# Cosformer attention and a token mixer: twenty products on constant data in six gaps of TensorE, and PSUM banks handed out anew

## The chip, the cores and the metric

One core of a Trainium2 chip. The metric is device time in microseconds (us) of one execution; lower is better. Times in this text count from the start of the profiled span.

## The reference

Two stages, one after the other, on 8 batches, 8 heads, 576 positions and 64 columns a head.

```python
def phi(x, c, s):
    r = np.maximum(x, 0.0)
    return np.concatenate([r * c, r * s], axis=-1)
q_p = phi(q, cos_w, sin_w)
k_p = phi(k, cos_w, sin_w)
kv = np.einsum('bhsf,bhsd->bhfd', k_p, v)
z = np.sum(k_p, axis=2)
num = np.einsum('bhsf,bhfd->bhsd', q_p, kv)
den = np.einsum('bhsf,bhf->bhs', q_p, z)[..., None] + 1e-06
...
wq = x @ w_q
wk = x @ w_k
W_tok = scale * np.einsum('bsd,btd->bst', wq, wk)
mixed = np.einsum('bst,btd->bsd', W_tok, x)
return (np.maximum(mixed, 0.0) @ w_out).astype(np.float32)
```

`x` is `num / den` with the heads side by side: 576 x 512 a batch. `cos_w` and `sin_w` depend on the position alone.

## The kernel before

The kernel has one written-out schedule, the string `ORDER` (lines 37 to 106). Each word is an operation with its arguments, then `@`, then the engine: T is TensorE (PE), V VectorE (DVE), A ScalarE (ACT), G GpSimd (POOL), Y SyncE (SP). For T the number after the letter is the first PSUM bank. `run` (line 440) goes through the words and calls the function of that name. An engine executes its own words in this order; between engines, the framework adds semaphores where one operation needs data or a buffer from another. So the string sets each engine's queue and the banks, and the data sets the rest.

The work is cut by H = 2b + h (b the batch, h one half of its eight heads, so H runs from 0 to 15) and by s, one of the two head pairs in such a half; g = 2H + s numbers the 32 head pairs. A word's numbers are H and s, or g, or b and a part of it. The steps:

- LD (line 203): loads one pair of k, q or v, 288 KB each, into one of four raw buffers, all from SP. It waits until the operation that read that buffer four halves earlier is done.
- RK (224) and MK (229): relu of k, then the product with cosine and sine (DVE). CV (237) casts v, DQ (242) makes relu of q twice side by side (POOL).
- QK (254): 18 products of k' with v and a column of ones, then 18 transposes of q, into two banks. EK (275) copies the first to SBUF, EQ (278) multiplies the second by cosine and sine; both on DVE.
- NM (288): 10 products of q' with kv. RC (299) is the reciprocal of the denominator, XN (307) the division; both on DVE.
- XT (318) and EX (331): 20 transposes of x, and their copy.
- A batch then goes through WQK, EW, DW, TK, EWK, KX, EKX, MX, EMX (lines 339 to 403: the mixer's products and the copies that read them), WO and EO (409, 417: the last product, four of 512 columns each, and its copy), and ST (422), the store. LW and CW (211, 218) load and cast the weights.

Ahead of all this stand 14 products of a constant tile `warm` (set to 1.0, line 451) with itself, 128 x 128 by 128 x 512, into bank 7, whose result nobody reads (lines 452 and 453).

TensorE's eight banks are shared by all operations: QK, NM, XT, WQK and MX take two banks, TK, KX and WO one. An operation has to wait until the last reader of its banks is done.

The start of TensorE's queue is QK.0, QK.1, NM.0, QK.3, NM.3, QK.2, QK.5, NM.1, NM.2, XT.1, NM.5, QK.4, XT.0, QK.6, NM.4, WQK.0, XT.2, TK.0, QK.7, QK.11, NM.6, KX.0, NM.7, and four MX. DVE's part beside it is EQ.0, EK.0, MK.1.1, EQ.1, RC.0, EK.1, EQ.3, EK.3, XN.0, MK.2.0, MK.2.1, RC.3, EQ.2, EK.2, XN.3, EK.5, RC.2, RC.1, XN.2, EQ.5, XN.1, MK.3.0, MK.3.1, EQ.4, EK.4, RC.5, EK.6, RC.4, MK.5.1, XN.4, XN.5.

Of the kernel before, what the change touches and what calls it, by code (L numbers as in the profile page):

```python
# [44 lines left out]
NM.2@T4 LW.qk@Y EK.5@V DQ.2.0@G RC.2@V RC.1@V LD.v.5.1@Y XN.2@V CV.3.0@G EQ.5@V LD.q.5.1@Y
XT.1@T2 XN.1@V LD.q.5.0@Y RK.3.0@A NM.5@T0 QK.4@T4 RK.3.1@A MK.3.0@V LD.k.5.0@Y XT.0@T6 CV.3.1@A
MK.3.1@V EX.1@A LD.v.4.0@Y EQ.4@V LD.q.4.0@Y EK.4@V RK.5.1@A RC.5@V QK.6@T2 LD.v.5.0@Y EX.0@A
NM.4@T4 EK.6@V CW.qk@G LD.q.4.1@Y RC.4@V RK.4.0@A MK.5.1@V WQK.0@T6 LD.k.4.1@Y CV.5.1@A DQ.3.1@G
XN.4@V LD.v.4.1@Y XN.5@V EW.0@A DQ.5.1@G LW.o@Y EQ.6@V DW.0@A XT.2@T0 TK.0@T4 LD.k.6.0@Y
MK.4.0@V QK.7@T6 EX.2@A QK.11@T2 EWK.0@V CV.4.0@G LD.k.6.1@Y EK.7@V EQ.7@V NM.6@T4 RK.5.0@G  # L50
LD.q.6.0@Y KX.0@T0 RC.6@V DQ.5.0@G XN.6@V NM.7@T6 LD.v.6.0@Y EKX.0@A CV.5.0@A DQ.4.0@G MX.0.2@T0
RC.7@V LD.k.7.0@Y MX.0.3@T4 EQ.11@V EMX.0.3@A EK.11@V LD.q.6.1@Y EMX.0.2@A MK.5.0@V MX.0.0@T4
MX.0.1@T2 RK.4.1@A QK.8@T0 LD.v.7.0@Y CV.4.1@G XN.7@V EMX.0.0@A DQ.4.1@G EQ.8@V EMX.0.1@A
XT.3@T6 QK.10@T4 EK.8@V EX.3@A MK.4.1@V NM.8@T0 EQ.10@V QK.9@T2 CW.o.0@G CW.o.1@A LD.v.6.1@Y
EK.10@V WQK.1@T6 EQ.9@V LD.q.7.0@Y RK.6.0@G EK.9@V NM.10@T4 RC.8@V LD.k.7.1@Y EW.1@A MK.6.0@V
WO.0.2@T2 LD.k.8.1@Y DQ.6.0@G RC.10@V NM.9@T6 XN.8@V EO.0.2@A WO.0.1@T3 LD.v.8.0@Y RK.6.1@A
XN.10@V CV.6.0@G TK.1@T2 EO.0.1@A LD.v.7.1@Y RK.7.0@G RC.9@V QK.12@T0 EWK.1@A XN.9@V DQ.6.1@G
LD.q.7.1@Y NM.11@T4 WO.0.0@T2 RC.11@V LD.k.8.0@Y MK.6.1@V KX.1@T3 EO.0.0@A LD.q.8.0@Y MK.7.0@V
DW.1@A WO.0.3@T6 CV.6.1@G EQ.12@V LD.k.9.0@Y EKX.1@A CV.7.0@A DQ.7.0@G MX.1.1@T2 EK.12@V
LD.v.10.0@Y XN.11@V EO.0.3@A QK.13@T0 EMX.1.1@A RK.7.1@G MX.1.0@T6 LD.k.9.1@Y QK.14@T4 EQ.13@V  # L60
EMX.1.0@A RK.8.1@G XT.4@T2 LD.v.8.1@Y EK.13@V EK.14@V MX.1.2@T6 MK.7.1@V WO.1.1@T0 EMX.1.2@A
LD.q.9.0@Y MK.8.1@V EX.4@A NM.12@T6 LD.q.8.1@Y WO.1.2@T1 DQ.7.1@G EQ.14@V EO.1.1@A LD.q.9.1@Y
RC.12@V XT.5@T2 CV.7.1@A RK.8.0@G XN.12@V NM.13@T4 LD.v.9.0@Y EX.5@A WO.1.0@T0 CV.8.0@G RC.13@V
DQ.8.0@G LD.k.10.1@Y XN.13@V MX.1.3@T6 RK.9.0@A QK.15@T2 LD.k.10.0@Y MK.8.0@V EO.1.2@A WQK.2@T4
EO.1.0@A MK.9.0@V LD.q.10.0@Y EMX.1.3@A CV.10.0@G EQ.15@V NM.14@T0 LD.v.9.1@Y EW.2@A QK.16@T6
RK.9.1@G RC.14@V CV.8.1@A EK.15@V LD.q.10.1@Y TK.2@T4 XN.14@V NM.15@T2 EWK.2@A WO.1.3@T5 DW.2@A
DQ.8.1@G LD.k.12.0@Y EQ.16@V EK.16@V LD.q.11.1@Y XT.6@T0 RC.15@V DQ.9.1@G QK.17@T6 EX.6@A
XN.15@V LD.k.11.1@Y KX.2@T4 CV.9.0@G EQ.17@V XT.7@T2 RK.10.1@G EKX.2@A EK.17@V EO.1.3@A EX.7@V
DQ.9.0@G MX.2.1@T0 NM.17@T6 EMX.2.1@A MX.2.0@T4 RC.17@V WQK.3@T2 EMX.2.0@A MK.9.1@V RK.10.0@A
CV.9.1@G XN.17@V MX.2.2@T0 QK.18@T4 EW.3@A LD.k.14.0@Y MK.10.1@V WO.1.4@T6 EMX.2.2@A ST.1.0.0@Y  # L70
MK.10.0@V LD.v.11.1@Y MX.2.3@T0 QK.19@T2 DW.3@G EQ.18@V ST.1.1.1@Y EMX.2.3@A TK.3@T7 DQ.10.0@G
EK.18@V ST.0.0.0@Y EK.19@V EWK.3@A NM.16@T0 EQ.19@V EO.1.4@A NM.18@T4 ST.1.0.1@Y WO.2.1@T7
DQ.10.1@G RC.16@V RC.18@V LD.k.11.0@Y XN.16@V QK.20@T2 ST.0.0.1@Y EO.2.1@A DQ.11.1@G XN.18@V
RK.12.0@A LD.v.10.1@Y KX.3@T0 RK.11.1@A CV.11.1@G LD.q.11.0@Y EQ.20@V NM.19@T4 EKX.3@A
LD.v.11.0@Y XT.8@T6 EK.20@V RC.19@V MX.3.1@T0 ST.0.1.0@Y EX.8@A MK.12.0@V WO.2.0@T2 LD.v.12.0@Y
XN.19@V RK.11.0@G WO.2.3@T3 LD.k.12.1@Y EMX.3.1@A MK.11.1@V ST.1.1.0@Y EO.2.0@A MX.3.2@T4
XT.9@T0 MK.11.0@V LD.v.12.1@Y QK.23@T6 EO.2.3@A LD.q.12.0@Y CV.10.1@G EX.9@V EMX.3.2@A NM.20@T2
ST.0.1.1@A DQ.11.0@G EK.23@V MX.3.3@T4 EQ.23@V WQK.4@T0 CV.11.0@A LD.q.13.1@Y RC.20@V EMX.3.3@A
LD.q.12.1@Y XN.20@V QK.22@T6 EW.4@A QK.21@T4 LD.k.13.0@Y EQ.22@V TK.4@T0 MX.3.0@T2 EK.21@V
RK.12.1@G ST.1.2.1@A WO.2.2@T1 EK.22@V EQ.21@V EWK.4@A LD.k.13.1@Y NM.23@T6 EMX.3.0@A MK.12.1@V  # L80
NM.22@T4 LD.v.13.1@Y EO.2.2@A KX.4@T0 RC.23@V RK.14.0@G CV.12.0@A XN.23@V NM.21@T2 ST.1.2.0@Y
DQ.12.0@G EKX.4@A WO.3.3@T1 RC.22@V LD.q.13.0@Y RC.21@V CV.12.1@G XN.22@V WO.3.0@T0 EO.3.3@A
LD.v.13.0@Y XN.21@V DW.4@A XT.11@T4 DQ.12.1@G ST.2.0.0@Y QK.24@T6 EX.11@V MX.4.2@T2 LD.q.14.0@Y
WO.3.2@T1 EMX.4.2@A EQ.24@V RK.13.0@G EO.3.0@A LD.v.14.0@Y EK.24@V MX.4.0@T2 MK.14.0@V QK.25@T4
EMX.4.0@A LD.k.15.0@Y MX.4.3@T6 RK.13.1@G WO.3.1@T0 EK.25@V EO.3.2@A EQ.25@V DQ.13.1@G
LD.k.14.1@Y EMX.4.3@V XT.10@T2 EO.3.1@A ST.2.0.1@Y MX.4.1@T4 WO.3.4@T1 MK.13.0@V EMX.4.1@A
ST.3.1.0@Y MK.13.1@V NM.24@T6 EO.3.4@A WO.4.0@T0 LD.v.15.0@Y CV.13.0@G RC.24@V EX.10@A XN.24@V
DQ.13.0@G NM.25@T4 LD.q.15.0@Y WO.4.1@T1 RC.25@V EO.4.0@A LD.k.15.1@Y CV.13.1@G XN.25@V QK.26@T2
EO.4.1@A DQ.14.0@G LD.q.14.1@Y QK.27@T6 CV.14.0@A EQ.26@V XT.12@T0 LD.v.14.1@Y RK.15.0@A
QK.28@T4 EK.26@V EK.27@V EX.12@A EQ.27@V RK.14.1@G ST.3.2.1@Y WQK.5@T2 EK.28@V LD.q.15.1@Y  # L90
MK.14.1@V WO.4.2@T6 EW.5@A MK.15.0@V ST.2.1.0@Y NM.27@T0 DW.5@G EQ.28@V EO.4.2@A NM.26@T2
TK.5@T7 CV.15.0@G RC.27@V EWK.5@A NM.28@T4 RC.26@V DQ.15.0@G WO.4.3@T6 XN.27@V RK.15.1@A RC.28@V
KX.5@T7 XN.26@V EO.4.3@A DQ.14.1@G QK.30@T0 EKX.5@A ST.4.1.1@Y XN.28@V MX.5.3@T2 MX.5.1@T6
LD.v.15.1@Y CV.14.1@G EQ.30@V EMX.5.3@A XT.13@T4 ST.4.1.0@Y EMX.5.1@A EK.30@V QK.29@T2 EX.13@V
ST.3.0.1@Y ST.2.1.1@A DQ.15.1@G MX.5.0@T0 NM.30@T6 EK.29@V ST.3.0.0@Y EMX.5.0@A EQ.29@V WQK.6@T4
ST.4.0.1@Y ST.3.1.1@A RC.30@V MK.15.1@V WO.5.0@T0 ST.3.2.0@Y EW.6@A XN.30@V CV.15.1@G ST.4.0.0@Y
NM.29@T2 DW.6@G TK.6@T1 RC.29@V MX.5.2@T4 QK.31@T6 EWK.6@V EMX.5.2@A XN.29@V KX.6@T1 EO.5.0@A
EK.31@V WO.5.4@T4 EQ.31@V ST.5.0.0@Y EKX.6@V NM.31@T2 ST.5.0.1@Y MX.6.0@T0 RC.31@V MX.6.1@T6
EMX.6.0@A WO.5.2@T5 XN.31@V EO.5.4@A EMX.6.1@V XT.14@T0 EO.5.2@A XT.15@T2 WO.5.3@T4 EX.14@V
EX.15@V WO.6.0@T5 EO.5.3@A WQK.7@T0 ST.5.2.0@A ST.5.2.1@Y EO.6.0@V WO.6.1@T2 EW.7@V MX.6.3@T4  # L100
DW.7@G MX.6.2@T0 EO.6.1@A TK.7@T3 EMX.6.2@V WO.5.1@T6 EWK.7@A ST.6.0.1@Y EMX.6.3@A ST.6.0.0@A
KX.7@T7 EO.5.1@V WO.6.3@T0 EKX.7@V ST.5.1.0@A ST.5.1.1@Y MX.7.1@T2 MX.7.3@T4 MX.7.0@T6 EMX.7.1@A
WO.6.2@T1 EMX.7.0@V EO.6.3@A EMX.7.3@V MX.7.2@T2 EO.6.2@A WO.7.1@T6 EMX.7.2@A ST.6.1.0@Y
WO.7.2@T7 ST.6.1.1@A EO.7.1@V WO.7.4@T0 EO.7.2@A WO.7.3@T1 ST.7.1.0@Y ST.7.1.1@A EO.7.4@V
# [404 lines left out]
```

## Time and profile before

| what | value |
|---|---|
| median of 13 runs | 132.45 us (130.33 to 134.48) |
| the profiled execution: its time, its span | 134.1 us, 132.3 us |
| TensorE (PE) busy | 104.5 us, 79% |
| VectorE (DVE) busy | 106.6 us, 81% |
| ScalarE (ACT) busy | 77.5 us, 59% |
| GpSimd (POOL) busy | 69.9 us, 53% |
| mean granted clock of TensorE | 0.912 of full |
| DMA | 39.40 MB, 298 GB/s on average |
| the 14 opening products | 1.45 to 7.25 us |

How to read it: the profile is one execution. The page cuts the span into 40 slices of 3.3 us; a digit is a busy share in tenths, and in the row PEclk the clock that TensorE was granted, in tenths of the full one. A time line row is the start, the time taken, the engine, line and operation, how many, and in square brackets how long the engine was idle before and what ended it. A row of the table of stages is a stretch of time with each engine's busy time in it, then the granted clock, the share of time that the DMA engines were busy, and GB/s. A row of waits names the engine and line that waited, the one that it waited for, the us in total, the times and the longest.

### The profile page before, as it was taken

The numbers are of one execution on the slowest core, as the hardware profiler recorded it, in microseconds if no ns is written. First come the engines' busy times: TensorE is split into PE (matmuls) and PEld (weight loads), VectorE is DVE, ScalarE is ACT, GpSimd is POOL, SyncE is SP. The second block draws the span as 40 slices with busy tenths as digits, with TensorE's granted clock in tenths as the row PEclk, the third lists the DMA queues.
The fourth block names the chain that finished last, engine by engine and source line by source line (L and its number), as shares of the span: only waits on it lengthen the run. The fifth ranks groups of instructions, "written<-read, shape, count | busy, mean of one in ns | idle before, by whom it ended". The sixth has DMA issues, their size and how long they took to land.

```text
span 132.3 us, 5180 instructions
## 1 busy us (share of the span) xinstructions
PE 104.5 (79%) x2181; PEld 69.7 (53%) x2198; DVE 106.6 (81%) x227; ACT 77.5 (59%) x124; POOL 69.9 (53%) x81
## 2 busy tenths in 40 slices
PE   5937695949789988869999869399998959999900
...
DVE  3648999798899999999999874999998967865500
...
PEclk9995555586899999999999999999999999999995
DMA  4999999999999999970299999999994998059793
GB/s 128 322 396 402 392 388 360 361 390 389 384 394 390 385 387 388 387 266 0 68 265 307 318 376 341 366 306 340 353 352 171 279 262 244 18 185 281 181 282 104
DMA packets 20711, 39.40 MB, mean 298 GB/s; under 512 B 3280, under 2 KB 3280, under 8 KB 20688
## 3 DMA queue, kind: packets, MB, share of 16 engines
...
q8 instruction: 17, 0.28, 0.9%
...
## 4 chain that ended last, share of the span: by engine, by line
DVE 35%; PE 30%; DMA 10%; SPq 8%; issue 6%; ACT 3%; POOL 2%; ACTq 2%; POOLq 0%
DVE kp L232 13%; PE banks L413 9%; DVE qpt L279 8%; DVE xs L309 7%; DMA kf<-in_k_dram 6%; SPq L208 5%; PE banks L260 4%; PE banks L292 4%; DMA qf<-in_q_dram 4%; PE banks L269 4%; PE banks L371 3%; SPq L430 3%; DVE rec L305 3%; DVE kvs L187 2%; PE banks L326 2%
## 5 line engine op out<-in xcount | busy, mean ns | idle before, releaser
L195 POOL TENSOR_SCALAR qd<-qf 128x1152 bf16<-128x1152 f32 x32 | 39.6, 1247 | 11.9 <-DMA qf<-in_q_dram 11.0
L413 PE MATMUL banks<-wo_sb,mix 128*128 128x512 bf16 x127 | 33.9, 380 | 1.3 <-issue 0.6
L232 DVE TENSOR_TENSOR kp<-rk,cossin 128x1152 bf16<-128x1152 bf16 x32 | 29.6, 944 | 2.7 <-POOL rk L195 2.3
L185 ACT COPY osb<-banks 128x512 f32<-128x512 f32 x31 | 18.0, 589 | 14.4 <-PE banks L413 9.2
L309 DVE TENSOR_TENSOR xs<-banks,rec 128x640 bf16<-128x640 f32 x32 | 25.4, 807 | 0.3
L279 DVE TENSOR_TENSOR qpt<-banks,cst 128x1152 bf16<-128x1152 bf16 x32 | 23.8, 745 | 1.9 <-PE banks L269 1.7
L401 ACT ACTIVATE mix<-banks 128x640 bf16<-128x640 f32 (+1 forms) x27 | 17.4, 656 | 10.3 <-PE banks L388 10.1
L260 PE MATMUL banks<-vb,kp 64*128 64x65 bf16 x576 | 16.7, 202 | 4.8 <-POOL vb L189 1.4
L292 PE MATMUL banks<-kvs,qpt 128*128 128x65 bf16 x320 | 16.5, 205 | 3.0 <-DVE kvs L187 2.1
L413 PEld LDWEIGHTS <-mix 128*128 128x128 bf16 x144 | 12.2, 98 | 12.5 <-issue 1.4
L269 PE MATMUL banks<-ident,qd 64*128 64x64 bf16 x576 | 16.3, 203 | 2.5 <-POOL qd L195 2.5
L260 PEld LDWEIGHTS <-kp 64*128 64x128 bf16 x576 | 13.3, 101 | 8.7 <-issue 4.3
L292 PEld LDWEIGHTS <-qpt 128*128 128x128 bf16 x320 | 14.1, 104 | 7.0 <-DVE qpt L279 2.1
L189 POOL TENSOR_SCALAR vb<-vf 128x576 bf16<-128x576 f32 x17 | 12.6, 741 | 6.6 <-DMA vf<-in_v_dram 5.5
L193 ACT ACTIVATE rk<-kf 128x576 bf16<-128x576 f32 x15 | 10.1, 684 | 9.1 <-DMA kf<-in_k_dram 7.4
L195 POOL TENSOR_SCALAR rk<-kf 128x576 bf16<-128x576 f32 x14 | 10.9, 782 | 7.7 <-DMA kf<-in_k_dram 6.5
L269 PEld LDWEIGHTS <-qd 64*128 64x128 bf16 x576 | 13.0, 103 | 2.6 <-POOL qd L195 2.6
L185 ACT COPY xT<-banks 128x1280 bf16<-128x1280 bf16 x10 | 12.3, 1226 | 3.5 <-PE banks L326 3.5
L326 PE MATMUL banks<-ident,xs 64*128 64x64 bf16 x320 | 7.9, 196 | 6.2 <-DVE xs L309 6.2
L185 ACT CAST vb<-vf 128x576 bf16<-128x576 f32 x14 | 9.4, 673 | 5.3 <-DMA vf<-in_v_dram 5.0
L189 POOL TENSOR_SCALAR wq<-wqk 64x576 bf16<-64x576 bf16 x4 | 3.0, 744 | 15.8 <-ACT wqk L185 8.0
L326 PEld LDWEIGHTS <-xs 64*128 64x128 bf16 x320 | 6.4, 99 | 9.3 <-DVE xs L309 6.1
...
## 6 DMA issues: line engine op xcount, KB each, us to landing
...
```

What stands on the lines that cost most here:

```text
L185: A.copy(dst, src)
L189: eng.tensor_scalar(dst, src, 1.0, 1.0, op0=ALU.mult, op1=ALU.mult)
L195: eng.tensor_scalar(dst, src, FMAX, 0.0, op0=ALU.min, op1=ALU.max)
L232: eng.tensor_mul(kp[H % N_KP][:, lo:hi], rk[H % N_RK][:, lo:hi].unsqueeze(3).to_broadcast([P, n, C9, 2, D]), cossin.unsqueeze(1).to_broadc ...
L260: T.matmul(kvp[:, hh, :], kp[H % N_KP][p0:p0 + 64, i, c, :, :], vb[H % N_VB][p0:p0 + 64, i, c, 0:D + 1], start=(c == 0), stop=(c == C9 - 1))
L269: T.transpose(qt[:, hh, c * D:(c + 1) * D], src, ident[p0:p0 + 64, p0:p0 + 64])
L279: eng.tensor_mul(qpt[g % N_QPT][:, :, 1:SLOTS, :], qk_views(at["QK", g])[0].rearrange("f h (c d) -> f h c d", c=C9), cst.unsqueeze(1).to_b ...
L292: T.matmul(nv[:, hh, u, :], qpt[g % N_QPT][:, hh, 2 * u:2 * u + 2, :], kvs[g % N_KV][:, hh, :], start=(u == 0), stop=(u == SC - 1 and not ...
L309: eng.tensor_tensor(xs[b % N_XS][:, :, 2 * pr:2 * pr + 2, :].rearrange("p u h d -> p h u d"), num_view(at["NM", g])[:, :, :, 0:D], rec[g % ...
L326: T.transpose(xv[:, r, i, u, :], xs[b % N_XS][p0:p0 + 64, u, 2 * hp:2 * hp + 2, :], ident[p0:p0 + 64, p0:p0 + 64])
L401: A.activation(dst, src, AF.Relu, scale=scale_moe)
L413: T.matmul(o, mix[b // 2 % N_MIX][:, dmc, base:base + P], wo_sb[:, dmc, :], start=(dmc == 0), stop=(dmc == NDM - 1))
```

## The change

A new operation WU issues n products of the constant tile into one bank, and six words of it stand in `ORDER`, all on TensorE: five products after QK.0, three before QK.3, six before NM.3, four before QK.5, one before NM.5 and one before MX.0.2. Nobody reads what they write; QK, NM or MX write over it. Without the WU words the order of each of the five engines is the same as before, and that of the loads and stores too. The banks of many operations from TK.0 on have other numbers. The rest of the string differs only in how the engines' words lie between each other. A line on `SPLIT` moves two lines down.

```diff
 LD.v.0.1@Y RK.1.0@V MK.1.0@V RK.0.0@V LD.v.1.1@Y LD.v.1.0@Y CV.0.0@V RK.0.1@A LD.q.2.1@Y
-MK.0.0@V LD.q.1.0@Y MK.0.1@V LD.k.2.0@Y DQ.0.0@G LD.k.2.1@Y LD.v.2.1@Y RK.1.1@V DQ.0.1@G QK.0@T0
-CV.0.1@A LD.v.2.0@Y EQ.0@V DQ.1.1@G QK.1@T2 CV.1.1@A LD.q.3.0@Y EK.0@V MK.1.1@V NM.0@T0 CV.1.0@A
-LD.q.2.0@Y EQ.1@V QK.3@T4 DQ.2.1@G LD.v.3.0@Y RC.0@V EK.1@V LD.k.3.1@Y EQ.3@V DQ.1.0@G EK.3@V
-LD.k.3.0@Y RK.2.0@A XN.0@V NM.3@T2 QK.2@T4 LD.v.3.1@Y RK.2.1@A MK.2.0@V MK.2.1@V CV.2.1@A
-LD.k.4.0@Y RC.3@V QK.5@T0 CV.2.0@A LD.k.5.1@Y EQ.2@V NM.1@T6 EK.2@V DQ.3.0@G LD.q.3.1@Y XN.3@V
...
+MK.0.0@V LD.q.1.0@Y MK.0.1@V LD.k.2.0@Y DQ.0.0@G LD.k.2.1@Y LD.v.2.1@Y RK.1.1@V QK.0@T0 CV.0.1@A
+LD.v.2.0@Y DQ.0.1@G WU.5@T2 EQ.0@V CV.1.1@A LD.q.3.0@Y EK.0@V DQ.1.1@G QK.1@T2 CV.1.0@A
+LD.q.2.0@Y NM.0@T0 MK.1.1@V LD.v.3.0@Y WU.3@T4 DQ.2.1@G EQ.1@V LD.k.3.1@Y QK.3@T4 RC.0@V WU.6@T6
+EK.1@V LD.k.3.0@Y RK.2.0@A DQ.1.0@G EQ.3@V LD.v.3.1@Y RK.2.1@A EK.3@V XN.0@V NM.3@T2 CV.2.1@A
+LD.k.4.0@Y QK.2@T4 MK.2.0@V WU.4@T6 CV.2.0@A LD.k.5.1@Y MK.2.1@V RC.3@V DQ.3.0@G LD.q.3.1@Y
+QK.5@T0 EQ.2@V NM.1@T6 LW.qk@Y EK.2@V XN.3@V DQ.2.0@G NM.2@T4 LD.v.5.1@Y EK.5@V RC.2@V CV.3.0@G
+RC.1@V LD.q.5.1@Y XN.2@V LD.q.5.0@Y RK.3.0@A EQ.5@V XT.1@T2 RK.3.1@A WU.1@T4 XN.1@V LD.k.5.0@Y
+NM.5@T0 CV.3.1@A QK.4@T4 MK.3.0@V LD.v.4.0@Y EX.1@A XT.0@T6 MK.3.1@V LD.q.4.0@Y EQ.4@V RK.5.1@A
...
+XN.5@V LD.k.6.0@Y EQ.6@V CV.4.0@G LD.k.6.1@Y XT.2@T0 TK.0@T7 QK.7@T4 EX.2@A MK.4.0@V LD.q.6.0@Y
+QK.11@T2 EWK.0@V RK.5.0@G LD.v.6.0@Y EK.7@V EQ.7@V NM.6@T6 DQ.5.0@G KX.0@T1 LD.k.7.0@Y RC.6@V
+NM.7@T4 XN.6@V EKX.0@A DQ.4.0@G LD.q.6.1@Y WU.1@T0 CV.5.0@A MX.0.2@T0 RC.7@V MX.0.3@T6 EQ.11@V
...
+    def WU(eng, pb, n):
+        for _ in range(n):
+            T.matmul(bank1(pb, 0, 2048, FP32), warm[:, 0:P], warm, start=True, stop=True)
+
-    ops = dict(LD=LD, LW=LW, CW=CW, RK=RK, MK=MK, CV=CV, DQ=DQ, QK=QK, EK=EK, EQ=EQ,
+    ops = dict(WU=WU, LD=LD, LW=LW, CW=CW, RK=RK, MK=MK, CV=CV, DQ=DQ, QK=QK, EK=EK, EQ=EQ,
```

Some of the new banks: QK.7 goes from 6 to 4, QK.14 from 4 to 2, XT.4 from 2 to 6, QK.27 from 6 to 2 and XT.12 from 0 to 4.

More of the change, by code (lines that the diff above doesn't have):

```diff
@@ L29 @@
 LD_PAIR = True
-SPLIT = (0, 1, 2, 3, 4, 5, 6, 7, 8, 9, 10, 11, 12, 13, 14, 15)
 UNITS = (((0, 1), (2, 3)), ((0,), (1, 2), (3, 4)))
 UNITS7 = ((0,), (1, 2), (3,), (4,))
+SPLIT = (0, 1, 2, 3, 4, 5, 6, 7, 8, 9, 10, 11, 12, 13, 14, 15)
 N_FIRST, N_WARM = 9, 14
@@ L45 @@
[L45 to L104, printed above, removed]
@@ L105 @@
-WO.7.0@T2 ST.7.3.0@A EO.7.3@V ST.7.3.1@A ST.7.2.0@Y EO.7.0@A ST.7.2.1@Y ST.7.0.0@A ST.7.0.1@Y
+MK.0.0@V LD.q.1.0@Y MK.0.1@V LD.k.2.0@Y DQ.0.0@G LD.k.2.1@Y LD.v.2.1@Y RK.1.1@V QK.0@T0 CV.0.1@A
[3 more added lines that the diff above has]
+LD.k.4.0@Y QK.2@T4 MK.2.0@V WU.4@T6 CV.2.0@A LD.k.5.1@Y MK.2.1@V RC.3@V DQ.3.0@G LD.q.3.1@Y
@@ new lines @@
+QK.5@T0 EQ.2@V NM.1@T6 LW.qk@Y EK.2@V XN.3@V DQ.2.0@G NM.2@T4 LD.v.5.1@Y EK.5@V RC.2@V CV.3.0@G
+RC.1@V LD.q.5.1@Y XN.2@V LD.q.5.0@Y RK.3.0@A EQ.5@V XT.1@T2 RK.3.1@A WU.1@T4 XN.1@V LD.k.5.0@Y
+NM.5@T0 CV.3.1@A QK.4@T4 MK.3.0@V LD.v.4.0@Y EX.1@A XT.0@T6 MK.3.1@V LD.q.4.0@Y EQ.4@V RK.5.1@A
+QK.6@T2 LD.v.5.0@Y EK.4@V EX.0@A RC.5@V CW.qk@G LD.q.4.1@Y NM.4@T4 EK.6@V RC.4@V DQ.3.1@G
+RK.4.0@A LD.k.4.1@Y WQK.0@T6 CV.5.1@A LD.v.4.1@Y MK.5.1@V EW.0@A DQ.5.1@G XN.4@V LW.o@Y DW.0@A
+XN.5@V LD.k.6.0@Y EQ.6@V CV.4.0@G LD.k.6.1@Y XT.2@T0 TK.0@T7 QK.7@T4 EX.2@A MK.4.0@V LD.q.6.0@Y
@@ new lines @@
+QK.11@T2 EWK.0@V RK.5.0@G LD.v.6.0@Y EK.7@V EQ.7@V NM.6@T6 DQ.5.0@G KX.0@T1 LD.k.7.0@Y RC.6@V
+NM.7@T4 XN.6@V EKX.0@A DQ.4.0@G LD.q.6.1@Y WU.1@T0 CV.5.0@A MX.0.2@T0 RC.7@V MX.0.3@T6 EQ.11@V
+LD.v.7.0@Y EMX.0.3@A CV.4.1@G EK.11@V EMX.0.2@A MX.0.0@T6 MK.5.0@V MX.0.1@T2 RK.4.1@A QK.8@T0
+DQ.4.1@G XN.7@V EMX.0.0@A EMX.0.1@A EQ.8@V XT.3@T4 LD.v.6.1@Y CW.o.0@G QK.10@T6 EK.8@V EX.3@A
+LD.q.7.0@Y NM.8@T0 MK.4.1@V CW.o.1@A LD.k.7.1@Y EQ.10@V RK.6.0@G QK.9@T2 LD.k.8.1@Y EK.10@V
+DQ.6.0@G WQK.1@T4 EQ.9@V LD.v.8.0@Y EK.9@V NM.10@T6 RC.8@V CV.6.0@G EW.1@A WO.0.2@T3 LD.v.7.1@Y
@@ new lines @@
+MK.6.0@V LD.q.7.1@Y NM.9@T4 EO.0.2@A RC.10@V RK.7.0@G WO.0.1@T2 XN.8@V RK.6.1@A LD.k.8.0@Y
+DQ.6.1@G TK.1@T3 XN.10@V EO.0.1@A QK.12@T0 LD.q.8.0@Y EWK.1@A CV.6.1@G RC.9@V NM.11@T6
+LD.k.9.0@Y XN.9@V WO.0.0@T3 DQ.7.0@G LD.v.10.0@Y RC.11@V KX.1@T2 EO.0.0@A MK.6.1@V LD.k.9.1@Y
+DW.1@A WO.0.3@T5 MK.7.0@V EKX.1@A LD.v.8.1@Y CV.7.0@A EQ.12@V RK.7.1@G MX.1.1@T2 LD.q.9.0@Y
+EO.0.3@A RK.8.1@G EK.12@V XN.11@V EMX.1.1@A QK.13@T0 LD.q.8.1@Y DQ.7.1@G MX.1.0@T4 QK.14@T2
+EQ.13@V LD.q.9.1@Y EMX.1.0@A XT.4@T6 RK.8.0@G EK.13@V EK.14@V LD.v.9.0@Y MX.1.2@T4 WO.1.1@T1
@@ new lines @@
+MK.7.1@V EMX.1.2@A LD.k.10.1@Y EX.4@A MK.8.1@V NM.12@T4 WO.1.2@T0 CV.8.0@G EQ.14@V LD.k.10.0@Y
+EO.1.1@A RC.12@V DQ.8.0@G XT.5@T6 LD.q.10.0@Y CV.7.1@A XN.12@V NM.13@T2 WO.1.0@T1 EX.5@A
+LD.v.9.1@Y RC.13@V XN.13@V MX.1.3@T4 LD.q.10.1@Y RK.9.0@A QK.15@T6 MK.8.0@V EO.1.2@A LD.k.12.0@Y
+WQK.2@T2 MK.9.0@V EO.1.0@A LD.q.11.1@Y EMX.1.3@A CV.10.0@G EQ.15@V NM.14@T0 EW.2@A LD.k.11.1@Y
+QK.16@T4 RC.14@V RK.9.1@G CV.8.1@A EK.15@V TK.2@T3 XN.14@V DQ.8.1@G NM.15@T6 EWK.2@A WO.1.3@T2
+DW.2@A EQ.16@V DQ.9.1@G EK.16@V XT.6@T0 RC.15@V QK.17@T4 EX.6@A XN.15@V CV.9.0@G KX.2@T3 EQ.17@V
@@ new lines @@
+XT.7@T6 RK.10.1@G EKX.2@A EK.17@V EO.1.3@A EX.7@V MX.2.1@T0 DQ.9.0@G NM.17@T4 EMX.2.1@A
+MX.2.0@T2 RC.17@V WQK.3@T6 EMX.2.0@A MK.9.1@V RK.10.0@A CV.9.1@G XN.17@V MX.2.2@T0 QK.18@T2
+EW.3@A LD.k.14.0@Y MK.10.1@V EMX.2.2@A WO.1.4@T5 ST.1.0.0@Y MK.10.0@V LD.v.11.1@Y MX.2.3@T0
+QK.19@T6 DW.3@G EQ.18@V ST.1.1.1@Y EMX.2.3@A TK.3@T4 EK.18@V DQ.10.0@G ST.0.0.0@Y EK.19@V
+EWK.3@A NM.16@T0 EQ.19@V EO.1.4@A NM.18@T2 ST.1.0.1@Y WO.2.1@T4 RC.16@V DQ.10.1@G LD.k.11.0@Y
+RC.18@V XN.16@V ST.0.0.1@Y QK.20@T6 EO.2.1@A DQ.11.1@G XN.18@V LD.v.10.1@Y RK.12.0@A KX.3@T5
```

32 lines of the change are left out of this document (added).

## The prediction

> **What bounds the kernel now.** I read the page's 40 slices first, then the time line of TensorE, then a table of stages cut at the moments where the clock changes, then the waits of the SP queue.
>
> The slices: VectorE (DVE) is busy nearly all the time from slice 4 on; TensorE's granted clock is at half in slices 3 to 7 and low again near 9.
>
> ```profile
> PE   5937695949789988869999869399998959999900
> DVE  3648999798899999999999874999998967865500
> PEclk9995555586899999999999999999999999999995
> DMA  4999999999999999970299999999994998059793
> ```
>
> The stage table (length, PE busy, PEld, DVE, ACT, POOL, then the granted clock, DMA share, GB/s):
>
> ```profile
> 6.77:10.19 3.42, 0.94 (x20) 0.34 (x18) 1.71 (x3) 0.68 (x1) 1.00 (x1) 1.00 1.04 396
> 10.19:13.60 3.41, 2.65 (x72) 2.30 (x74) 2.96 (x5) 2.02 (x3) 3.24 (x4) 0.50 1.05 401
> 13.60:17.01 3.41, 2.36 (x74) 2.21 (x72) 3.26 (x9) 2.42 (x4) 1.89 (x2) 0.50 1.05 391
> 17.01:20.43 3.42, 2.79 (x72) 2.38 (x66) 3.05 (x9) 0.29 (x1) 1.75 (x2) 0.50 1.05 391
> 23.84:27.25 3.41, 3.20 (x77) 2.58 (x72) 2.56 (x9) 3.41 (x5) 1.26 (x2) 0.50 1.06 380
> 27.25:30.66 3.41, 1.57 (x55) 1.25 (x54) 3.41 (x5) 1.64 (x4) 3.04 (x4) 1.00 1.05 390
> 81.86:85.27 3.41, 1.36 (x6) 0.44 (x5) 3.27 (x9) 1.26 (x2) 1.94 (x3) 1.00 1.01 356
> ```
>
> The clock steps on a grid of 3.41 us. It falls after a stage with little work (0.94, 1.57 us busy), comes back after one that is nearly full (3.20 us), and stays low after 2.79 us (82%). It is at half for 17.07 us from 10.19 and 3.41 us from 30.66.
>
> But the slow TensorE costs little, since DVE hardly waits for it. DVE's time line shows 1.1 us of such idle time before 26.9: 0.26 before RC.2 (20.11), 0.06 before RC.1, 0.48 before EK.6 (25.88), 0.30 before RC.4 (26.48); and 0.94 us later (0.39 before EK.7 at 31.78, 0.21 and 0.34 before RC.6 and RC.7). That is the most that an earlier full clock can give back on DVE. TensorE's time line shows how small the gaps are at the places of the first four insertions:
>
> ```profile
> 7.47 0.46 PE L260 MATMUL banks<-vb,kp 64*128 64x65 bf16 x18 [0.22 <-DVE kp L232]
> 10.39 0.66 PE L269 MATMUL banks<-ident,qd 64*128 64x64 bf16 x18 [2.46 <-POOL qd L195]
> 11.34 0.68 PE L260 MATMUL banks<-vb,kp 64*128 64x65 bf16 x18 [0.29 <-ACT vb L185]
> 13.43 0.68 PE L260 MATMUL banks<-vb,kp 64*128 64x65 bf16 x18 [0.26 <-DVE kp L232]
> 15.64 0.71 PE L292 MATMUL banks<-kvs,qpt 128*128 128x65 bf16 x10 [1.05 <-DVE kvs L187]
> 17.70 0.68 PE L260 MATMUL banks<-vb,kp 64*128 64x65 bf16 x18 [0.27 <-DVE kp L232]
> ```
>
> Does a shift at 27 us reach the end? DMA is full until 57 us and then lies idle for 8 us, because a load waits for compute:
>
> ```profile
> SPq L208 <- ACT rk L193: 8.6, 1, 8.6
> ```
>
> That is LD.k.14.0 behind RK.10.0 on ACT (63.53), which follows TensorE and DVE; the chain goes on from it through SP's issues to a load that lands at 80.9. DVE's idle time from 37.5 to 64.8 is only about 0.55 us, so I carry a shift at 27 us to the end at full size.
>
> [...] The trace's 14 opening products took 5.80 us, 0.41 each, the last two straddling the step at 6.78; twelve products of line 413 in a row took 2.71 us, 0.23 each. So I price a product at 0.43 cold and 0.22 warm. [...] 1.57 us with transposes let the clock fall, 1.36 us of full products did not. [...]
>
> **The change part by part.** The order on each of the five engines and of every DMA is the same word for word, apart from six insertions on TensorE; no queue is passed by anything. What each engine waits for is otherwise the same, so I go through the insertions, at the grid of this trace.
>
> *Five products after QK.0.* The large gap (2.46 us, before QK.0's transposes, which wait for q) comes ahead of them and stays. QK.0 ends at 11.05, five cold products cost 5 × 0.43 = 2.13, and QK.1 starts at 13.2 in place of 11.34. The stage from 10.19 is now busy for 3.2 of 3.41 us, so I take the clock back at 13.60. A QK takes 1.15 us cold (the one from 13.43) and 0.72 warm (from 36.16), so QK.1 ends near 14.1; EQ.1 on DVE moves from 13.30 to 14.1. Behind EQ.1 stand RC.0, EK.1 and EQ.3. NM.0 warm (0.31) ends at 14.4.
>
> *Three before QK.3:* 0.65 warm, to 15.05; QK.3 to 15.75. EQ.3 starts at 15.8, before 14.63: **DVE is 1.15 us late**, the price of eight products less the cover there.
>
> *Six before NM.3:* 1.3 warm, to 17.05. NM.3 would wait for EK.3 until 16.65 anyway, and RC.3 is behind XN.0 and two MK on DVE (to 18.8): hidden. Without that cover it costs 0.4.
>
> *Four before QK.5:* QK.2 ends at 18.1, in time for EQ.2 (19.05), the products at 18.95, and QK.5 needs MK.2.1 (18.8): 0.15, hidden, as EK.5 comes only at 20.8. NM.2, now warm and ready at 20.3, no longer holds RC.2: 0.32 of the 1.15 comes back, and RC.2 starts at 21.0, 0.85 late by RC.1.
>
> *One before NM.5:* bank 4 was read last by XN.2, which XT.1 needs too, so no new wait; 0.22 under NM.5's wait for EQ.5. *One before MX.0.2:* bank 0 was read by EX.2 (until 31.6); 0.22, of which 0.18 can fall on ACT at EMX.0.3, covered by ACT's idle 0.70 before EW.1 (40.66). Without the covers, 0.2 each.
>
> Then TensorE waits from 20.3 to 22.3 for XN.2, and the clock may fall again at 23.84. Either way EK.6, right behind RC.5, starts at 26.25 (before 25.88; 0.48 comes back) and RC.4 at 26.55 at the latest (before 26.48). With the clock still full it would be 0.1 early. Two points pull both kernels together there: RK.3.0 waits for k until 21.5, and WQK.0 for CW.qk, whose weights land at 25.9; neither moves. From 28 to 29.9 TensorE idles as before, and the clock falls at 30.66 as before.
>
> *Banks.* By the new numbers every operation follows the same earlier user of its bank or an older one in nearly all places (QK.7 moves to the banks of NM.4, whose reader XN.4 XT.2, ahead of QK.7, waits for anyway). QK.14 and QK.27 now follow MX.1.1 and NM.25 three operations back. QK.14 started at 48.42 and EMX.1.1 ends near 48.5, so 0.1 on TensorE, under EQ.14's start at 51.93. The longest wait for a bank's reader in this trace (MX.0.0 for ACT) was 0.7 us, so the bounds are −0.7 to +0.7; I take 0, since XT.4 and XT.12 gain what these two lose.
>
> Sum: 2.13 + 0.65 for eight products, less 1.63 (the gaps of 0.29 and 0.26, and QK.1, NM.0 and QK.3 running faster), = 1.15; less 0.32, 0.48 and 0.28 of DVE's idle time = about **+0.1 us**. The profiled execution has a span of 132.3 and a time of 134.1, so 132.4 and 134.2; the median of the runs is 132.45, 1.65 lower, and I move that by the same amount: **132.6**. About 1% (1.3 us) is what a measurement of this kernel can tell from no change.
>
> **Rivals.**
>
> *B, the window falls late.* With the grid shifted, the stage that holds the five products may begin before 9.5 and be too empty; the clock comes back one boundary later, at 15.1 to 16.8. Then EQ.3 is 1.8 to 2.55 late, 1.1 comes back by 26.9, and +0.7 to +1.45 stays: 133.15 to 133.9, middle 133.5. [...]
>
> *C, the clock never falls.* With a boundary near 8.9, the stage before it holds enough of the opening products, and the one after it the five. Then everything is warm: EQ.0 is 0.25 early, RC.2 0.5, RC.4 1.0, and the second fall can be missed, which gives the 0.94 too: −1.9, 130.55. POOL doesn't forbid it: QK.8 (36.16) has its q at 33.9. Against it: 0.94 us in a stage let the clock fall here.
>
> *D, the products don't lift the clock*, because they and the small products together don't count enough by 17.0. It decides if the clock is still at half there. Up to 20.4 then: QK.3 ends at 17.4, six cold products take 2.56, QK.2 ends at 21.2 and EQ.2 is 3.4 late; after 0.85 back +2.5: 134.95, slower. (With no lift at all RC.2 would be 5.8 late: 137.) Against it: the 14 opening products, on the same data, did lift the clock after one full stage.
>
> **How the numbers follow.** My case 0.52, B 0.26, C 0.14, D 0.08. Slower by over 1%: D, the upper part of B (0.10) and 0.06 of downstream scatter, 0.24. Faster by over 1%: most of C and a little scatter, 0.14. Within: 0.62. The range 130.9 to 134.3 takes in B whole and the near half of C, and leaves out D; my case alone is 131.9 to 133.1.
>
> **What would show it.** Right: clock at half from about 10.2 for only one or two stages; EQ.3 1 to 2.5 us later than 14.63; no idle time on DVE before RC.2 and EK.6; RC.4 within 0.3 us of 26.5 (or 0.7 to 1.4 late in B); RK.10.0 shifted by the same. Wrong: EQ.3 not late (the gaps did cover the products), a shift at RC.4 that is gone at RK.10.0 or grown, a new wait of TensorE for a bank after 36 us.

## The result and the profile after

| | before | after |
|---|---|---|
| median of the runs | 132.09 us (48 runs, 130.24 to 134.48) | 134.09 us (11 runs, 131.79 to 138.73) |
| ratio | | 1.014 (95%: 1.008 to 1.020) |
| profiled execution: time, span | 134.1, 132.3 us | 132.45, 130.7 us |
| mean granted clock | 0.912 | 0.965 |

The change made the kernel slower by 1.4%. A ratio here is taken over executions within 1.5% of the fastest of their kernel; since some of these kernels scatter by 5%, the medians of all executions stand beside it below.

The profiled execution is no typical one: at 132.45 us it is faster than ten of the eleven timed ones, and its clock is full for nearly the whole time. Its 40 slices:

```profile
PE   5917985398679968869999868899699879999910
DVE  3659999897999999999999857999999987865500
PEclk9999999959999999999999976999999999999996
DMA  4999999999999999990189999999994799359794
```

The half clock of slices 3 to 7 is gone, what is left of it is one stage near slice 8 (and one near slice 24). In the table of stages, cut at this execution's own grid (columns as before):

```profile
5.38:8.79 3.41, 1.65 (x24) 0.67 (x22) 2.17 (x3) 0.68 (x1) 0.00 (x0) 1.00 1.03 386
8.79:12.21 3.42, 1.72 (x42) 1.05 (x45) 2.16 (x4) 1.47 (x3) 3.08 (x3) 1.00 1.04 407
12.21:15.62 3.41, 3.36 (x84) 2.06 (x78) 3.38 (x8) 1.71 (x3) 3.05 (x3) 1.00 1.05 392
22.45:25.86 3.41, 1.57 (x76) 1.30 (x68) 2.88 (x10) 3.41 (x5) 0.40 (x1) 1.00 1.10 340
25.86:29.27 3.41, 3.08 (x39) 1.94 (x40) 3.41 (x5) 2.04 (x4) 2.93 (x4) 0.50 1.04 383
73.65:77.06 3.41, 1.82 (x24) 1.32 (x23) 2.95 (x7) 1.10 (x3) 1.82 (x2) 1.00 0.97 331
```

A boundary lay at 8.79: the stage before it holds 1.65 us of work, the one after it the five products, and the clock held through both. It fell only at 25.86, after 1.57 us of small products, and at 77.06, after 1.82 us. This is rival C's grid. TensorE's time line at the places of the first four insertions (a row "x4" or "x2" lacks a record or two):

```profile
10.34 0.44 PE L270 MATMUL banks<-ident,qd 64*128 64x64 bf16 x18 [2.26 <-POOL qd L196]
10.93 1.03 PE L435 MATMUL banks<-warm 128*128 128x512 bf16 x4 [0.16 <-issue]
11.89 0.46 PE L261 MATMUL banks<-vb,kp 64*128 64x65 bf16 x18
13.08 0.59 PE L435 MATMUL banks<-warm 128*128 128x512 bf16 x2
14.26 1.47 PE L435 MATMUL banks<-warm 128*128 128x512 bf16 x6
15.56 0.47 PE L293 MATMUL banks<-kvs,qpt 128*128 128x65 bf16 x10
16.84 0.81 PE L435 MATMUL banks<-warm 128*128 128x512 bf16 x3 [0.16 <-issue]
```

At full clock a product costs 0.22 (the starts of the three from 16.84 lie 0.215 and 0.216 apart), and the insertions fit: EQ.3 on DVE starts at 14.37 (before 14.63), RC.4 at 25.42 (before 26.48). Here, too, MK.5.1 is shorter than in the kernel before, 0.93 against 1.56 (both lines below). But the lead does not last. EQ.8 is 2.0 us early (35.17 against 37.16), EQ.12 0.6 (46.06 against 46.69), and the load behind RK.10.0 also goes out 0.6 us early (63.59 against 64.23):

```profile
SPq L209 <- ACT rk L194: 7.4, 1, 7.4
```

Where the 1.4 us went is in DVE's time line, at two products with cosine and sine (MK). First two lines of the kernel before, then three of the changed one:

```profile
16.23 1.41 DVE L232 TENSOR_TENSOR kp<-rk,cossin 128x1152 bf16<-128x1152 bf16 x2
...
26.81 1.56 DVE L232 TENSOR_TENSOR kp<-rk,cossin 128x1152 bf16<-128x1152 bf16 x1
```

```profile
25.75 0.93 DVE L233 TENSOR_TENSOR kp<-rk,cossin 128x1152 bf16<-128x1152 bf16 x1
...
36.03 1.55 DVE L233 TENSOR_TENSOR kp<-rk,cossin 128x1152 bf16<-128x1152 bf16 x1
...
43.94 2.20 DVE L233 TENSOR_TENSOR kp<-rk,cossin 128x1152 bf16<-128x1152 bf16 x2
```

and in POOL's, in the same stretch:

```profile
35.93 1.05 POOL L190 TENSOR_SCALAR wo_sb<-wo_f 128x1024 bf16<-128x1024 f32 x1 [0.41 <-DMA wo_f<-in_moe_w_out_dram]
...
44.36 2.31 POOL L196 TENSOR_SCALAR rk<-kf 128x576 bf16<-128x576 f32 x2
```

MK.4.1 came early enough to meet POOL's cast of the weights and took 1.55; in the kernel before it ran at 38.02 in 0.74. MK.6.1 and MK.7.0 took 2.20 in place of 1.73. 0.81 + 0.47 = 1.3 of the 1.4 us.

The trace of the kernel before is no typical one either: at 134.1 us it is the second slowest of the 48 executions, so differences from it flatter the changed kernel.

So the traced execution explains why a lucky grid gains little, not why the median is 2 us worse. For that I needed other grids.

### The profile page after: what moved, and what is told of

Its sections match the earlier page's. It is cut to its first block, busy times and chain, and to the rows that moved or that the text cites. A ratio compares the mean times of both kernels' runs of the same rounds, so it can differ in the third digit from the quotient of the medians.

```text
span 130.7 us, 5222 instructions
## 1 busy us (share of the span) xinstructions
PE 104.0 (80%) x2196; PEld 67.3 (52%) x2218; DVE 107.7 (82%) x227; ACT 77.5 (59%) x124; POOL 70.1 (54%) x81
## 4 chain that ended last, share of the span: by engine, by line
DVE 35%; PE 27%; DMA 8%; issue 8%; SPq 7%; POOL 6%; ACT 4%; ACTq 2%; POOLq 0%
DVE kp L233 12%; PE banks L414 10%; DVE qpt L280 8%; DVE xs L310 8%; SPq L209 5%; DMA qf<-in_q_dram 4%; DMA vf<-in_v_dram 4%; POOL qd L196 3%; PE banks L344 3%; PE banks L261 3%; PE banks L270 3%; DVE rec L306 3%; SPq L431 2%; PE banks L372 2%; PE banks L293 2%
## 5 line engine op out<-in xcount | busy, mean ns | idle before, releaser
L414 PE MATMUL banks<-wo_sb,mix 128*128 128x512 bf16 x127 | 34.1, 382 | 1.4 <-issue 0.8
L233 DVE TENSOR_TENSOR kp<-rk,cossin 128x1152 bf16<-128x1152 bf16 x32 | 30.6, 976 | 1.4 <-POOL rk L196 1.2
L280 DVE TENSOR_TENSOR qpt<-banks,cst 128x1152 bf16<-128x1152 bf16 x32 | 23.8, 744 | 1.9 <-PE banks L270 1.7
L261 PE MATMUL banks<-vb,kp 64*128 64x65 bf16 x576 | 15.4, 194 | 6.9 <-DVE qpt L280 1.4
L261 PEld LDWEIGHTS <-kp 64*128 64x128 bf16 x576 | 12.3, 96 | 11.3 <-issue 2.9
L270 PE MATMUL banks<-ident,qd 64*128 64x64 bf16 x576 | 15.1, 193 | 3.3 <-POOL qd L196 2.3
L293 PE MATMUL banks<-kvs,qpt 128*128 128x65 bf16 x320 | 14.7, 194 | 2.1 <-DVE kvs L188 1.1
L293 PEld LDWEIGHTS <-qpt 128*128 128x128 bf16 x320 | 12.6, 97 | 5.7 <-issue 1.6
L196 POOL TENSOR_SCALAR rk<-kf 128x576 bf16<-128x576 f32 x14 | 11.6, 834 | 7.2 <-DMA kf<-in_k_dram 6.8
L270 PEld LDWEIGHTS <-qd 64*128 64x128 bf16 x576 | 11.6, 96 | 3.9 <-POOL qd L196 2.4
L344 PE MATMUL banks<-xT,wqk_sb 128*128 128x288 bf16 x64 | 10.1, 306 | 1.4 <-POOL wqk_sb L190 0.8
L188 DVE CAST kvs<-banks 128x130 bf16<-128x130 f32 x32 | 8.7, 280 | 1.5 <-PE banks L270 1.5
```

Source lines behind the costliest of these rows:

```text
L196: eng.tensor_scalar(dst, src, FMAX, 0.0, op0=ALU.min, op1=ALU.max)
L233: eng.tensor_mul(kp[H % N_KP][:, lo:hi], rk[H % N_RK][:, lo:hi].unsqueeze(3).to_broadcast([P, n, C9, 2, D]), cossin.unsqueeze(1).to_broadc ...
L261: T.matmul(kvp[:, hh, :], kp[H % N_KP][p0:p0 + 64, i, c, :, :], vb[H % N_VB][p0:p0 + 64, i, c, 0:D + 1], start=(c == 0), stop=(c == C9 - 1))
L270: T.transpose(qt[:, hh, c * D:(c + 1) * D], src, ident[p0:p0 + 64, p0:p0 + 64])
L280: eng.tensor_mul(qpt[g % N_QPT][:, :, 1:SLOTS, :], qk_views(at["QK", g])[0].rearrange("f h (c d) -> f h c d", c=C9), cst.unsqueeze(1).to_b ...
L293: T.matmul(nv[:, hh, u, :], qpt[g % N_QPT][:, hh, 2 * u:2 * u + 2, :], kvs[g % N_KV][:, hh, :], start=(u == 0), stop=(u == SC - 1 and not ...
```

## The experiments

Theory A: the products cost DVE time when they run at half clock, which depends on where the clock's grid of stages falls. Theory B: the new banks add waits. Theory C: the loss arises after 36 us, whatever the clock did early. (These letters are not those of the prediction's rivals.) All kernels compute the whole result. Each group of runs has the kernel before measured beside it on the same chip; the groups were on different chips.

**Banks alone, products alone, the first five alone.** The edits, as words of `ORDER`:

```diff
 # e1, from the changed kernel
-WU.5@T2  -WU.3@T4  -WU.6@T6  -WU.4@T6  -WU.1@T4  -WU.1@T0
 # e2, from the kernel before (its banks)
+WU.5@T2 QK.1@T2 / +WU.3@T4 QK.3@T4 / +WU.6@T6 NM.3@T2 / +WU.4@T6 QK.5@T0 / +WU.1@T4 NM.5@T0 / +WU.1@T1 MX.0.2@T0
 # e4, from the kernel before
+WU.5@T2 QK.1@T2
```

Banks alone: 

> The changed kernel without its twenty products: only the banks are new. Theory A (the products are paid on TensorE when the clock comes back late): as before, ratio 0.995 to 1.005. Theory B (the new banks add waits after 36 us): slower, 1.01 to 1.02, as the whole change.

Products alone: 

> The kernel before with the twenty products at the same six places, old banks. Theory A: the whole loss, 1.01 to 1.02. Theory B: as before, 0.995 to 1.005, or a little faster, as the clock is full for longer.

The changed kernel again: 

> The changed kernel again, for a second trace, as the first one (time 132.45) is faster than nearly all of its runs. Time ratio 1.01 to 1.02 by both theories. Theory A: if the run is slow, its trace has the clock at half while the products run, and EQ.3 on DVE starts 1 to 2.5 us after 14.6. Theory B: EQ.3 near 14.6, and the loss stands after 36 us.

The first five: 

> The kernel before with the first five products alone, after QK.0. Theory A: they run at half clock more often than the rest do, so they carry a third to a half of the loss: 1.003 to 1.01. Theory B: 0.995 to 1.005.

Measured, with the kernel before at 131.48 (11 runs):

| kernel | median, range (6 runs) | ratio |
|---|---|---|
| banks alone | 132.02 (130.51 to 132.28) | 1.011 (1.003 to 1.019) |
| products alone | 133.69 (131.26 to 136.69) | 1.011 (0.997 to 1.024) |
| changed, again | 133.69 (131.09 to 137.22) | 1.012 (1.001 to 1.023) |
| first five | 132.31 (130.84 to 133.34) | 1.012 (1.002 to 1.022) |

The ratios don't tell the four apart: by them the banks alone (1.011) miss theory A's 0.995 to 1.005 and fall into B's range, and the first five (1.012) lie above A's. The medians and ranges do tell them apart. The products alone have the median of the whole change and its long tail, 2.2 us above the kernel before; the banks alone have neither and lie 0.5 us above it. So by the medians the products carry most of the loss. A small cost of the banks is not excluded. The first five alone lie 0.8 us above, which six runs don't separate from the banks' 0.5.

The trace of the products alone (133.52 us) is the one execution of the slower half that I have. The grid had boundaries at 9.37, 12.78 and 16.20, and the clock was at half from 9.37 to 16.20. TensorE's time line:

```profile
11.15 2.32 PE L434 MATMUL banks<-warm 128*128 128x512 bf16 x5
13.40 0.68 PE L260 MATMUL banks<-vb,kp 64*128 64x65 bf16 x18
...
15.03 1.38 PE L434 MATMUL banks<-warm 128*128 128x512 bf16 x3
16.35 0.46 PE L260 MATMUL banks<-vb,kp 64*128 64x65 bf16 x18
```

DVE's:

```profile
17.11 0.76 DVE L279 TENSOR_TENSOR qpt<-banks,cst 128x1152 bf16<-128x1152 bf16 x1 [1.28 <-PE banks L269]
...
18.72 2.38 DVE L232 TENSOR_TENSOR kp<-rk,cossin 128x1152 bf16<-128x1152 bf16 x2
...
25.76 1.83 DVE L232 TENSOR_TENSOR kp<-rk,cossin 128x1152 bf16<-128x1152 bf16 x2
```

and POOL's:

```profile
17.73 2.76 POOL L195 TENSOR_SCALAR qd<-qf 128x1152 bf16<-128x1152 f32 x2 [2.08 <-DMA qf<-in_q_dram]
```

The eight products take 2.3 + 1.4 us at half clock and EQ.3 waits 1.28 us for its QK: 17.11, 2.5 late. Being late, MK.2.0 and MK.2.1 now run beside POOL's DQ.3.0 and DQ.2.0, which start at 17.2 to 18.9 in all traces, mostly as q lands. The two MK take 2.38 in place of the 1.41 of before, another 1.0, and the next pair, MK.3.0 and MK.3.1, takes 1.83 in place of 1.41, another 0.4. RC.4 starts at 29.01 (+2.5), RK.10.0 at 64.90 (+1.4).

The changed kernel's second trace (132.0 us) has the clock full from 5.42 to the end: EQ.3 at 14.79, RC.4 at 25.86, EQ.12 at 46.32, RK.10.0 at 63.13. Full clock throughout, and no better than an ordinary run of the kernel before.

**Forcing the clock's state.** The number of opening products (`N_WARM`, 14) was set to 2, so that the clock should be at half when q arrives (in the two traces it was, until 16.24 and 24.3 us), or to 24, to bridge the wait for q, in both kernels.

```diff
-N_FIRST, N_WARM = 9, 14
+N_FIRST, N_WARM = 9, 2     # e5 changed, e6 before
+N_FIRST, N_WARM = 9, 24    # e7 changed, e8 before
```

Changed, 2: 

> The changed kernel with 2 opening products in place of 14, so that the clock is at half when q arrives[...]. Theory A (the products cost DVE time when they run at half clock): every run is slow, 133 to 137, ratio 1.02 to 1.035, and no run of 130; EQ.3 after 15.8, RC.4 over 27. Theory C (the loss is downstream of 36 us and has nothing to do with the early clock): as the changed kernel, 1.015, with the same scatter.

Before, 2: 

> The kernel before with 2 opening products. Theories A and C both: 0.997 to 1.005, as the clock was at half from 10.2 anyway and QK.0's first half waits for nothing that matters. If it is slower by over 1%, the opening products themselves matter and the run beside it must be read against this one.

Changed, 24: 

> The changed kernel with 24 opening products, which fill the wait for q at 8 to 10.3 us, so that the clock is full when the twenty products run. Theory A: the loss is gone, 130 to 132 in nearly all runs, ratio 0.985 to 1.0, mean clock above 0.96. Theory C: 1.01 to 1.02.

Before, 24: 

> The kernel before with 24 opening products alone. The clock is full at 10.3 us but the small products after it may not hold it: 0.99 to 1.003 by both theories. If it equals the changed kernel with 24, the twenty products add nothing even when the clock is full.

Measured, with the kernel before at 132.02 (61 runs):

| kernel | median, range (runs) | ratio |
|---|---|---|
| changed, 2 | 133.44 (131.21 to 135.6; 6) | 1.010 (0.999 to 1.021) |
| before, 2 | 131.99 (130.37 to 134.95; 22) | 0.999 (0.995 to 1.003) |
| changed, 24 | 132.37 (129.85 to 136.32; 22) | 1.002 (0.996 to 1.008) |
| before, 24 | 131.57 (129.69 to 135.2; 22) | 0.993 (0.990 to 0.997) |

With 24 opening products most of the loss is gone, which speaks for A and against C; what is left is 0.8 us over the kernel before with the same 24. But A's numbers were too strong on both sides. With 24, 9 of 22 runs took 132 or less, not nearly all. With 2, not every run is slow: the ratio of 1.010 misses A's 1.02 to 1.035, C's 1.015 lies in its interval, and the 1.45 us over the kernel before with the same 2 is no more than the 2.0 and 2.2 us with 14, on other chips. So forcing the clock to half at the start did not make the loss larger. Its trace (131.21 us) has the clock back at 16.24, EQ.3 at 16.89 and RC.4 at 27.41, as expected, and then EQ.12 at 46.82, where the kernel before has 46.69: a shift of 0.9 us that was gone 20 us later. With 24, the trace's grid had a boundary at 4.54, so the opening products ran at full clock from there, were over at 8.31, and left 1.8 us of waiting after all; the clock fell at 11.36, during the first five products. So this run does not show products at full clock, and why 24 help is not shown. The kernel before with 24 opening products and without the twenty is the fastest version that I found, 0.7% under the kernel before by its ratio, 0.3% by the medians; it was measured in one group of runs only.

**More draws, and twice the products.** Three single executions of the changed kernel, the last of them later, and four of it with the counts doubled:

```diff
-WU.5  WU.3  WU.6  WU.4  WU.1  WU.1
+WU.10 WU.6  WU.12 WU.8  WU.2  WU.2
```

Draw: 

> The changed kernel once more, one execution with a trace: half of its runs took over 133.5, and no trace of such a one is at hand. Theory A: if it is over 133.5, EQ.3 is later than 16 and RK.10.0 on ACT later than 64.5 (63.5 before). Theory C: it is over 133.5 with RK.10.0 below 63.5, and the loss lies after 64 us.

Draw: 

> The same again[...]. Expected as in the run beside it.

Doubled: 

> The changed kernel with twice the products in each of the six places (10, 6, 12, 8, 2, 2). Theory A: the loss grows by more than its own size, as another 20 products cost 20 x 0.22 = 4.4 us warm and 8.6 cold with no gaps left to hide them: 136 to 139, ratio 1.03 to 1.055, and RC.4 at 29 to 33. Theory C: 1.015 to 1.025.

A last draw: 

> The changed kernel once more, one execution with a trace, since the draws so far (132.45, 132.0, 132.83, 131.85) lie in the faster half of its runs. Theory A: if it is over 133.5, the clock is at half for two stages around the first products, EQ.3 is at 17 or later and RK.10.0 at 64.5 or later, as in the trace of the products with the old banks. Theory C: over 133.5 with EQ.3 before 16 and RK.10.0 below 63.5. If it is again under 133.5, the slowest executions stay without a trace.

Doubled: 138.37 us (138.18 to 138.92; 4 runs), ratio 1.055 (1.044 to 1.065), as A expects. TensorE's time line of it:

```profile
11.63 3.33 PE L435 MATMUL banks<-warm 128*128 128x512 bf16 x9 [0.33 <-issue]
14.90 0.46 PE L261 MATMUL banks<-vb,kp 64*128 64x65 bf16 x18
...
17.91 2.76 PE L435 MATMUL banks<-warm 128*128 128x512 bf16 x11
```

EQ.3 starts at 18.02, RC.4 at 31.23, RK.10.0 at 68.36: 3.4, 4.8 and 4.8 late. So large a delay does reach RK.10.0 in full. All but the first ten of these products ran at full clock (half from 10.7 to 14.1, and again from 34.6 to 38.0, when none of them ran), so this run shows that products beyond the gaps cost time, not that the half clock makes the loss of the twenty.

The draws took 132.83, 131.85 and 132.47 us: again none over 133.5, though 11 of 21 executions of the changed kernel are, and 9 of all 128 of the kernel before. What was expected of one over 133.5 was not put to the test. They do show three grids. Times in us, next to the other traces (the clock is also at half at the very start, before its first step up: in the trace of before until 6.76, with the opening products 0.427 us apart):

| trace | time | clock at half, before 36 us | EQ.3 | RC.4 | EQ.12 | RK.10.0 |
|---|---|---|---|---|---|---|
| before | 134.1 | 10.2 to 27.2, 30.7 to 34.1 | 14.63 | 26.48 | 46.69 | 63.53 |
| banks alone | 130.51 | 11.4 to 25.1 | 14.85 | 25.95 | 45.88 | 62.68 |
| changed, first | 132.45 | 25.9 to 29.3 | 14.37 | 25.42 | 46.06 | 62.89 |
| changed, second | 132.0 | none | 14.79 | 25.86 | 46.32 | 63.13 |
| changed, draw 1 | 132.83 | 28.7 to 32.1 | 13.94 | 25.32 | 46.20 | 63.02 |
| changed, draw 2 | 131.85 | 11.8 to 15.2 | 16.09 | 26.61 | 46.59 | 63.41 |
| changed, draw 3 | 132.47 | 11.2 to 14.6, 24.8 to 31.7 | 15.95 | 28.09 | 46.73 | 63.70 |
| products alone | 133.52 | 9.4 to 16.2, 29.9 to 33.3 | 17.11 | 29.01 | 47.87 | 64.90 |
| first five | 130.84 | 11.8 to 15.2, 18.7 to 25.5 | 14.93 | 26.20 | 45.76 | 62.60 |
| before, 2 | 132.45 | until 24.3, 34.6 to 38.0 | 14.25 | 25.40 | 45.70 | 62.92 |
| before, 24 | 131.86 | 17.0 to 23.8 | 14.03 | 25.11 | 46.02 | 62.85 |

RC.4 is spread over 3.9 us, EQ.12 over 2.2. The kernel before is late in its own trace: the four kernels without the full twenty products (banks alone and the last three rows) have EQ.12 at 45.7 to 46.0, the changed kernel's five traces at 46.1 to 46.7. Against those four, the changed kernel is up to 1.0 us late there. Draw 3 shows how a loss is made and given back. Its MK.2.0 and MK.2.1 meet POOL, and its MK.5.1, which in the kernel before ran beside POOL in 1.56, comes late enough to lie mostly between two instructions of POOL, and takes 0.72. DVE's time line:

```profile
15.95 0.76 DVE L280 TENSOR_TENSOR qpt<-banks,cst 128x1152 bf16<-128x1152 bf16 x1 [0.85 <-PE banks L270]
...
17.55 2.36 DVE L233 TENSOR_TENSOR kp<-rk,cossin 128x1152 bf16<-128x1152 bf16 x2
...
28.43 0.72 DVE L233 TENSOR_TENSOR kp<-rk,cossin 128x1152 bf16<-128x1152 bf16 x1
```

Whether these MK meet POOL depends on q as well as on DVE. In draw 2, EQ.3 is even later (16.09), but q landed 1.3 us later too, POOL started at 18.87 in place of 17.58, and the same two MK took 1.42:

```profile
17.69 1.42 DVE L233 TENSOR_TENSOR kp<-rk,cossin 128x1152 bf16<-128x1152 bf16 x2
```

Nor do the MK alone explain the loss: over a whole trace their mean length is 0.944 us in the kernel before, 0.969 with the banks alone and 0.944 to 0.976 in the five traces of the changed kernel.

And in the first row of the table, the second half of the span takes 0.7 to 2.4 us longer from RK.10.0 to the last copy than in the others (63.8 us against 61.4 to 63.1), with the same order of work; the traces of the changed kernel alone differ there by 1.3 us. Of these five, the two slowest there (63.0 and 63.1) have one more stage at half clock, at 77 to 80 and 80 to 83 us; the other three (61.7 to 62.2) have none. But the kernel before has none either, and takes 63.8. That scatter comes on top, and its cause is open.

The mean clock of every execution is on record. Of the 21 of the changed kernel, the two highest (0.996 and 0.993) took 131.09 and 132.0, the two lowest (0.921 and 0.924) took 138.73 and 137.24. But one of 137.22 had 0.958, in the midst of the others, and the kernel before ran within 134 us at clocks down to 0.883. So in the changed kernel a low clock goes with a long time, which fits theory A, but it is neither needed nor enough.

## Why the prediction was right and where it was wrong

The range (130.9 to 134.3) held the median of 134.09, in part by luck. The kernel before beside it came out at 132.09, 0.36 below the 132.45 from which the range was built; the change of +2.0 us is more than the +1.85 of its upper end, and no sum of the prediction gives it. The likeliest case, 132.6 and no change, did not come: the kernel is 1.4% slower, the case to which I gave 0.24.

*The price of a product and the length of the clock's stages* were right: 3.41 us, 0.43 us a product at half clock (2.32 for five), 0.22 at full. Both prices stand in the trace of before: its opening products start 0.427 us apart at half clock (cold in the prediction), the products of line 413 mostly 0.216 at full (warm). The window in the prediction and the expectations is a stage of the 3.41 us grid. How full a stage has to be was not settled by the stage table of before (see the last section), so the weights of my case and of B were my estimate.

*My own case* was right in its totals in one trace, and not by its own steps. Draw 2 has EQ.3 at 16.09 (15.8 predicted) and RC.4 at 26.61 (26.55 predicted), and DVE's idle time before RC.2, EK.6 and RC.4 was given back as I had summed it. But the clock fell at 11.8 and not at 10.2: QK.1 started at 12.30 and not at 13.2, and it was the three products, not the five, that ran almost wholly at half clock. The nearness of EQ.3 is luck. No trace of the changed kernel has the grid that I assumed, and I gave it half of the executions.

*Rival B* had its first steps right (EQ.3 1.8 to 2.55 late; measured 2.5 with the products alone). "1.1 comes back by 26.9" came true as well: the waits before RC.2, EK.6 and RC.4 are gone in that trace. Yet RC.4 was 2.5 late, and not 0.7 to 1.45. The step that failed is a term put at nothing, MK's: I took each at its length of before, and the two pairs that meet POOL there took 1.4 us more (2.38 and 1.83, in place of 1.41 each). I read the 1.56 of MK.5.1 in the time line of before as its length, and didn't ask why it was twice its neighbours'.

*Rival C's* gain of 1.9 was there at EQ.8 (2.0), again partly by luck: the second fall of the clock was not missed (25.86 to 29.27), and the waits behind it gave back 0.35 (0.15 and 0.44 left of 0.94). Another 0.63 came from the shorter MK.5.1, which the sum did not have. At the end the gain was gone. I had asked whether POOL's data would be ready (it was) and not whether DVE would run beside POOL's instructions. That C brings nothing fits with lucky grids not making up for the others.

*"I carry a shift at 27 us to the end at full size"* failed. In the traces of the banks alone, of the first five, of the kernel before with other openings, of the changed kernel and of it with 2, shifts between −1.4 and +1.6 at RC.4 were −1.0 to +0.1 at EQ.12. The 2.5 of the products alone kept 1.2 at EQ.12 and 1.4 at RK.10.0, the 1.7 of the changed kernel with 24 opening products 0.9 and 1.6, and only the 4.8 of the doubled ones reached RK.10.0 whole. The idle time of DVE, from which I argued, is not the only reserve: an MK beside POOL is longer by up to 0.95 us, so moving DVE against POOL takes up or gives back such pieces.

*The covers* of 0.22 before NM.5 and MX.0.2, and the banks, cost nothing that a trace shows. In the traces with the new banks an NM near 74 us waits for a copy on ACT (0.2 to 1.0 us), which the trace of before lacks; but the same wait stands with the old banks as well (0.5 with the first five, 0.8 with 2 opening products).

What stays open: why the median is 2 us worse, and the executions of 135 to 138.7 us. That the products cost the time is shown by the runs with and without them. How they do it is seen only as far as RC.4, in a few traces. Rival B with the MK's 1.4 added would give 134.6 to 135.3, an estimate that carries all of it to the end; the one trace of that kind took 133.52. I have no trace of an execution over 135 except of the doubled kernel; that those are grids with the products at half clock is argued from the 24 and the clocks on record, not shown, and the run with 2 speaks against it.
